# One-hot rows sent with the mask constants, identity sent alone, first head's rows copied on chip

## The chip, the cores and the metric

The kernel runs on one core of a Trainium2 chip. The metric is the device time of one execution in microseconds (us); lower is better. Three runs of the kernel before gave 269.93, 270.38 and 272.29 us, a median of 270.38 us. Engines are named as the profile names them: PE is the matrix engine (PEld is its weight load), DVE the vector engine, ACT the scalar engine, POOL the GpSimd engine, and SP the engine that does nothing here but issue transfers. ACT and POOL issue transfers as well, between their own work.

## The reference

The program is a block-sparse attention whose output goes through a token-and-channel mixer:

```python
scores = scale * np.matmul(q, k.transpose(0, 1, 3, 2))      # 4 batches, 8 heads, 768 x 64
mask = np.abs(blk_i - blk_j) <= 1                             # blocks of 32: the neighbours,
mask = mask | (blk_i == 0) | (blk_j == 0) | (blk_i == last) | (blk_j == last)
mask[qb's rows, kb's columns] = True                          # and three sampled blocks per row block
attn = softmax(np.where(mask, scores, -1e9))
x = concat_heads(attn @ v)                                    # 4 x 768 x 512
u = x + (x.T @ U @ V).T
out = u + np.maximum(u @ w_ch1, 0.0) @ w_ch2
```

The part that matters here is how the mask gets into the scores. There are 24 blocks of 32 tokens, so the mask is a 24 x 24 table. For the first batch the kernel adds it by widening the inner product: beside the 64 rows of a head's queries stand 24 rows that are one-hot (row i is 1 where the token lies in block i), and beside the 64 rows of its keys stand 24 rows that hold the bias of that key against each query block. One matrix product of 128 rows then gives score plus bias.

## The kernel before

Eight heads of a batch are worked in four pairs; there are sixteen pairs in all. For a pair the kernel turns queries and keys so that the head dimension lies on partitions, multiplies key tiles of 128 tokens by all 768 queries (lines 980, 999 and, from batch 1 on, 1030), takes the exponential on ACT (989, 1007, 1039), and multiplies by the values (414). The mixer's products (685, 760) are woven between. The order of all of that is written out by hand in a string of words (line 448 on), and each engine runs its instructions strictly in program order. Semaphores hold an instruction until what it needs is there.

The change lies in the prologue, lines 243 to 342, also in a fixed order. The tile `res` holds, for two sets, the widened queries `qres` and keys `kres` of two heads each: 128 partitions, 768 columns of 16-bit numbers per head. For head 0 of a pair, partitions 0 to 63 hold data and 64 to 87 the mask rows; for head 1 the data lies on 64 to 127 and the mask rows on 0 to 23. Unused rows are zero.

What the prologue does, engine by engine:

- SP issues the loads of head 0's queries and keys (line 182), then two copies of the one-hot rows from DRAM into set 0 (line 187, `one_hot(0, 1)` and `one_hot(0, 0)`), each behind the DVE memset of the rows that it writes into, then head 1's queries and keys, the values of pair 0, and pair 1's loads (153, 166). Later, in `second_set` (192 to 196), it writes set 1's one-hot rows, again from DRAM, copies the key mask rows from set 0, and fills `kmask`.
- ACT issues two transfers: `small` (line 245; a 128-row tile with the fixed part of the mask `ms`, the block numbers `iota` and a 128 x 128 identity `id16`), and the sampled blocks `sb` (246). Then it loads its function table and runs one small exponential (265).
- DVE zeroes five regions, casts head 0's queries (213), works out the mask bias from `sb`, `iota` and `ms` (302, 306, 309) and casts head 0's keys.
- POOL zeroes set 1 with two memsets over all 128 partitions (261), sets the columns of ones in the value tiles (263), and casts head 1's queries and keys when they land.
- PE runs eight products whose results nobody uses (`keep_warm`, 272), turns head 0's queries with `id16` (227), multiplies the bias by head 1's one-hot rows (`mask_half`, 279), turns the keys, and goes on to the first scores. ACT and DVE move these results out of PSUM (`first_row` 293, `mask_row` 287).

A transfer issued from SP or ACT takes one of eight semaphore lanes in turn, and its issue waits for the landing of the transfer eight places before it.

Of the kernel before, what the change touches and what calls it, by code (L numbers as in the profile page):

```python
# [12 lines left out]
FP32 = mybir.dt.float32  # L13
FP16 = mybir.dt.float16
# [5 lines left out]
P = 128  # L20
# [3 lines left out]
def kernel(  # L24
# [14 lines left out]
    nc = tc.nc  # L39

    B, H, S, D = q.shape
    BLK = 32
    NB = S // BLK
# [9 lines left out]
    MASK_BIAS = -240.0  # L53
# [3 lines left out]
    ii = np.arange(NB)  # L57
    ms_np = (
        (np.abs(ii[None, :] - ii[:, None]) <= 1)
        | (ii[None, :] == 0)  # L60
        | (ii[:, None] == 0)
        | (ii[None, :] == NB - 1)
        | (ii[:, None] == NB - 1)
    ).astype(np.float32)
    cols = np.arange(S)
    blk = ((cols % P) * T + cols // P) // BLK
    ohT_np = (blk[None, :] == ii[:, None]).astype(np.float16)
    small_np = np.zeros((P, NB + 1 + P // 2), np.float32)
    small_np[:NB, :NB] = (ms_np - 1.0) * -MASK_BIAS
    small_np[:NB, NB] = ii  # L70
    small_np[:, NB + 1 :] = np.eye(P, dtype=np.float16).view(np.float32)

    small_dr = nc.inline_tensor(small_np, name="small_const")
    ohT_dr = nc.inline_tensor(ohT_np, name="one_hot_const")

    consts = ctx.enter_context(tc.tile_pool(name="consts", bufs=1))
    wpool = ctx.enter_context(tc.tile_pool(name="wpool", bufs=1))
# [11 lines left out]
    def bank(n, shape, dtype):  # L89
        ap = PS[:, n, :]  # L90
        if dtype != FP32:
            ap = ap.bitcast(dtype)
        ap = ap[:, 0 : int(np.prod(shape[1:]))]
        return ap.rearrange("p (a b) -> p a b", a=shape[1]) if len(shape) > 2 else ap
# [3 lines left out]
    def psc2():  # L98
        ring["psc"] += 1
        return PS[:, (0, 3)[ring["psc"] % 2] :][:, 0:2]  # L100

    small = consts.tile([P, NB + 1 + P // 2], FP32)
    ms = small[0:NB, 0:NB]
    iota = small[0:NB, NB : NB + 1]
    id16 = small[:, NB + 1 :].bitcast(FP16)
    sb = consts.tile([P, NB, 3, 2], I32)
    vts = [consts.tile([P, H, T, DV], FP16, name=f"vt{i}") for i in range(2)]
    NEST = 16
# [3 lines left out]
    res = consts.tile([P, 4, 2, S], FP16, name="res")  # L112
    qres = [res[:, i] for i in range(2)]
    kres = [res[:, 2 + i] for i in range(2)]
    drows = [slice(0, D), slice(D, P)]
    mrows = [slice(D, D + NB), slice(0, NB)]
    hid = consts.tile([P, 2, 16, HS], FP16, name="hid")
# [58 lines left out]
    def first_load(h, n, queue):  # L176

        src, nm = ((q, "qld"), (k, "kld"))[n]
        if h == 0:
            lds[nm] = ldpool.tile([P, 2, T, D], FP32, tag="ld" + nm, name=nm)  # L180
            sts[0, nm] = stpool.tile([P, T, 2, D], FP16, tag="st" + nm, name="st" + nm)
        queue.dma_start(
            out=lds[nm][:, h], in_=src[0, h].rearrange("(p t) d -> p t d", t=T)
        )

    def one_hot(i, h):
        nc.sync.dma_start(out=qres[i][mrows[h], h, :], in_=ohT_dr.ap())

    warm = nc.const_aps.tensor(1.0, [P, 512], mybir.dt.bfloat16)
    bias = consts.tile([P, 2, D], FP16)  # L190

    def second_set():
        for h in range(2):
            one_hot(1, h)
            nc.sync.dma_start(out=kres[1][mrows[h], h, :], in_=kres[0][mrows[h], h, :])
        nc.sync.dma_start(out=kmask[mrows[0], :], in_=kres[0][mrows[0], 0, :])

# [13 lines left out]
    def first_cast(h, n, copy):  # L211
        nm = ("qld", "kld")[n]
        copy(out=sts[0, nm][:, :, h], in_=lds[nm][:, h])
# [3 lines left out]
    def first_turn(n, c):  # L217

        if n == 1:
            pt = bank(5 + c, [P, HS], FP32)  # L220
        elif c == 0:
            pt = pw[:, 1, 0:HS]
        else:
            pt = psc2()[:, 0, 0:HS]
        first_out[n, c] = pt
        for j in range(3):
            nc.tensor.matmul(
                pt[0:D, j * P : (j + 1) * P],
                sts[0, ("qld", "kld")[n]][:, 3 * c + j, 0],
                id16,  # L230
                start=(j == 0), stop=(j == 2), skip_group_check=True,
            )

    with tc.manual_schedule(
        engines={
            mybir.EngineType.PE,
            mybir.EngineType.DVE,
            mybir.EngineType.Activation,
            mybir.EngineType.SP,
            mybir.EngineType.Pool,  # L240
        }
    ):
        first_load(0, 0, nc.sync)
        first_load(0, 1, nc.sync)
        nc.scalar.dma_start(out=small, in_=small_dr.ap())
        nc.scalar.dma_start(
            out=sb[0:NB].rearrange("k z r w -> k (z r w)"),
            in_=sampled_blocks.bitcast(I32)
            .rearrange("z r -> (z r)")[None, :]
            .broadcast_to([NB, NB * 6]),  # L250
        )
        for h in (1, 0):
            nc.vector.memset(qres[0][(slice(D, P), slice(0, D))[h], h, :], 0.0)
            one_hot(0, h)
        nc.vector.memset(bias, 0.0)
        for h in range(2):
            nc.vector.memset(kres[0][(slice(D, P), slice(0, D))[h], h, :], 0.0)
        for n in range(2):
            first_load(1, n, nc.sync)
        for tile_ in (qres[1], kres[1]):  # L260
            nc.gpsimd.memset(tile_.bitcast(FP32), 0.0)
        for vt in vts:
            nc.gpsimd.memset(vt[:, :, :, D : D + 1], 1.0)
        first = consts.tile([P, 1], FP32)
        nc.scalar.activation(
            out=first, in_=nc.const_aps.tensor(1.0, [P, 1], FP32), func=AF.Exp
        )
        pw = psc2()

        def keep_warm(n, cols=512):  # L270
            for _ in range(n):
                nc.tensor.matmul(  # L272
                    pw[:, 0, 0:cols], warm[:, 0:P], warm[:, 0:cols], start=True, stop=True
                )

        pks = [bank(2, [P, HS], FP32), bank(7, [P, HS], FP32)]

        def mask_half(c):
            nc.tensor.matmul(
                pks[c],  # L280
                bias[0:NB].rearrange("k a z -> k (a z)"),
                qres[0][mrows[1], 1, c * HS : (c + 1) * HS],
                start=True, stop=True,
            )

        def mask_row(h, c, copy, lo=0, hi=HS):
            copy(
                out=kres[0][mrows[h], h, c * HS + lo : c * HS + hi],
                in_=pks[c][mrows[h], lo:hi],
            )  # L290

        def first_row(n, c, copy, lo=0, hi=HS):
            copy(
                out=(qres, kres)[n][0][drows[0], 0, c * HS + lo : c * HS + hi],
                in_=first_out[n, c][0:D, lo:hi],
            )

        neq = consts.tile([P, NB, 3], FP32)
        a01 = consts.tile([P, NB], FP32)
        keep_warm(8)  # L300
        first_cast(0, 0, nc.vector.tensor_copy)
        nc.vector.tensor_tensor(
            out=neq[0:NB], in0=sb[0:NB, :, :, 0],
            in1=iota[:, :, None].broadcast_to([NB, NB, 3]), op=ALU.not_equal,
        )
        nc.vector.tensor_reduce(
            out=a01[0:NB], in_=neq[0:NB], axis=mybir.AxisListType.X, op=ALU.min
        )
        nc.vector.scalar_tensor_tensor(
            out=bias[0:NB, :, 0:NB], in0=a01[0:NB, None].broadcast_to([NB, 2, NB]),  # L310
            scalar=MASK_BIAS, in1=ms[:, None].broadcast_to([NB, 2, NB]),
            op0=ALU.mult, op1=ALU.max,
        )
        first_turn(0, 0)
        first_row(0, 0, nc.scalar.copy)
        first_turn(0, 1)
        first_row(0, 1, nc.scalar.copy)
        first_cast(0, 1, nc.vector.tensor_copy)
        mask_half(0)
        mask_row(0, 0, nc.vector.tensor_copy, 0, P)  # L320
        mask_row(1, 0, nc.scalar.copy)
        first_turn(1, 0)
        first_row(1, 0, nc.vector.tensor_copy, 0, P)
        first_row(1, 0, nc.scalar.copy, P, HS)
        mask_row(0, 0, nc.vector.tensor_copy, P, HS)
        first_turn(1, 1)
        first_row(1, 1, nc.vector.tensor_copy)
        mask_half(1)
        mask_row(0, 1, nc.vector.tensor_copy)
        mask_row(1, 1, nc.vector.tensor_copy)  # L330

        for n in range(2):
            first_cast(1, n, nc.gpsimd.tensor_copy)
        for tile_ in (Vt, kmask):
            nc.gpsimd.memset(tile_.bitcast(FP32), 0.0)
        nc.vector.memset(Ut, 0.0)
        load_v(0)
        load_qk(1)
        load_v(1)
        load_mix_u()  # L340
        second_set()
        load_mix_v()

# [840 lines left out]
```

## Time and profile before

| what | value |
|---|---|
| profiled execution, its own time | 270.01 us |
| its span, first to last instruction | 268.2 us |
| runs: lowest, median, highest | 269.93, 270.38, 272.29 us |
| PE busy | 262.4 us, 98% of the span |
| DVE busy | 232.5 us, 87% |
| ACT busy | 202.7 us, 76% |
| POOL busy | 72.7 us, 27% |
| mean granted PE clock | 0.999 |

Busy time is the union of the intervals in which an engine has an instruction in flight. Products overlap in PE, so a busy PE need not be PE at its best. The profile also gives a chain of work that ended last: followed back from the last instruction, at each step to what released it. A timeline gives each instruction's start, its length, and in brackets the idle time before it and what ended that; SPq and ACTq rows are the issues of transfers. The trace also records every increment of a transfer's semaphore; the last of these is called its landing here. All times in a row count from the span's start.

### The profile page before, as it was taken

The page shows a single profiled execution, that of the slowest core. Times are in us where ns is not written, and L with a number is a line of the kernel's source. Part 1 is how long each engine was busy: PE and PEld are TensorE (multiplying, and loading weights), DVE is VectorE, ACT ScalarE, POOL GpSimd, SP SyncE. Part 2 cuts the span into 40 slices and gives each one's busy share as a digit, 9 for nine tenths or more (in the row PEclk, how much of TensorE's full clock was granted, in tenths as well). Part 3 has the DMA queues.
Part 4 walks back from the last instruction along what each step waited for, and adds up shares of the span by engine and source line. Part 5 has one row for each costly group of instructions (what it writes and reads, how often), then busy time and mean ns, then how long its engine had stood idle before and what let it go on. Part 6 is the DMA issues. An engine that isn't in the chain of part 4 may idle for free.

```text
span 268.2 us, 7303 instructions
## 1 busy us (share of the span) xinstructions
PE 262.4 (98%) x3006; PEld 182.4 (68%) x3006; DVE 232.5 (87%) x477; ACT 202.7 (76%) x265; POOL 72.7 (27%) x98
## 2 busy tenths in 40 slices
PE   8899999999999999999999999999999999999995
PEld 3677775555577778565666887555667788666884
DVE  5789988988999998868588997688998999999993
ACT  4999998897989667788898857788997944789200
POOL 4669006944462570070606160000000000000000
PEclk9999999999999999999999999999999999999999
DMA  6799997999999999897938997610200116400024
GB/s 192 245 324 263 207 235 123 113 135 144 189 146 133 117 103 111 284 98 89 90 39 67 106 109 139 223 34 13 51 0 2 42 42 117 159 2 0 2 98 137
DMA packets 88720, 31.66 MB, mean 118 GB/s; under 512 B 77104, under 2 KB 85840, under 8 KB 88688
## 3 DMA queue, kind: packets, MB, share of 16 engines
q0 software_dynamic: 49728, 10.10, 48.4%
q1 hardware_dynamic: 38492, 20.86, 33.6%
q8 instruction: 23, 0.38, 0.6%
q10 hardware_dynamic: 468, 0.26, 0.4%
q14 instruction: 9, 0.07, 0.1%
HBM read 27.67 MB, written 6.29 MB: 127 GB/s over the span
## 4 chain that ended last, share of the span: by engine, by line
PE 73%; DMA 12%; DVE 7%; ACT 2%; POOL 2%; issue 1%; SPq 0%; DVEq 0%; POOLq 0%; ACTq 0%
PE ps L760 32%; PE ps L685 17%; DMA w2t<-in_moe_w_ch_dram 9%; PE ps L414 9%; PE ps L1030 7%; DMA vld<-in_v_dram 2%; PE ps L999 2%; ACT est L1007 2%; PE ps L980 1%; DVE est L1045 1%; PE ps L272 1%; DMA qpl<-stqld 1%; PE ps L665 1%; DVE xf L551 1%; DVE res L969 1%
## 5 line engine op out<-in xcount | busy, mean ns | idle before, releaser
L1039 ACT ACTIVATE est<-ps 128x1536 f16<-128x1536 f32 x72 | 100.6, 1450 | 18.8 <-PE ps L1030 18.7
L685 PE MATMUL ps<-uT,w1t 128*128 128x384 f16 x384 | 70.2, 326 | 0.0
L1045 DVE TENSOR_TENSOR est<-est,mask 128x1440 f16<-128x1440 f16 x72 | 63.4, 903 | 0.6 <-ACT est L1039 0.2
L685 PEld LDWEIGHTS <-w1t 128*128 128x128 f16 x384 | 35.6, 97 | 26.6 <-issue 6.8
L414 PEld LDWEIGHTS <-est 128*128 128x128 f16 x1152 | 40.4, 97 | 7.0 <-issue 3.3
L414 PE MATMUL ps<-vt,est 128*128 128x65 f16 x1152 | 43.3, 193 | 0.2 <-DVE xf L551 0.2
L760 PEld LDWEIGHTS <-hid 128*128 128x128 f16 x358 | 34.0, 98 | 6.6 <-issue 1.6
L697 ACT ACTIVATE hid<-ps 128x384 f16<-128x384 f32 x63 | 29.7, 496 | 4.8 <-PE ps L685 4.3
L1030 PE MATMUL ps<-qpl,kpl 64*128 64x512 f16 (+1 forms) x288 | 31.7, 325 | 0.0
L139 POOL DMA_DIRECT2D stqld<-in_q_dram x20 | 16.3, 820 | 55.9 <-DMA qpl<-stqld 54.4
L760 PE MATMUL ps<-w2t,hid 128*128 128x256 f16 x238 | 31.1, 273 | 0.0
L879 DVE TENSOR_TENSOR xf<-xf,ps 128x256 f32<-128x256 f32 x63 | 25.4, 416 | 4.1 <-PE ps L760 3.7
L699 DVE TENSOR_SCALAR hid<-ps 128x384 f16<-128x384 f32 x33 | 18.3, 555 | 8.7 <-PE ps L685 8.0
L760 PEld LDWEIGHTS <-sums 128*128 128x128 f16 x216 | 20.1, 98 | 4.4 <-issue 1.0
L989 ACT ACTIVATE est<-ps 128x768 f16<-128x768 f32 x30 | 22.5, 812 | 0.1
L1030 PEld LDWEIGHTS <-kpl 64*128 64x128 f16 x288 | 12.3, 94 | 14.3 <-issue 9.1
L760 PE MATMUL ps<-res,sums 128*128 128x256 f16 x144 | 19.4, 273 | 0.0
L634 ACT CAST xh<-xf 128x384 f16<-128x384 f32 x24 | 11.0, 510 | 10.0 <-DVE xf L630 10.0
L551 DVE TENSOR_TENSOR xf<-ps,rcp 128x384 f32<-128x384 f32 x32 | 17.7, 554 | 0.8
L139 POOL DMA_DIRECT2D stkld<-in_k_dram x20 | 16.3, 819 | 1.9 <-issue 0.8
L139 POOL DMA_DIRECT2D vt<-in_v_dram x20 | 16.3, 820 | 0.0
L760 PE MATMUL ps<-res,hid 128*128 128x256 f16 x120 | 15.9, 273 | 0.0
(121 smaller groups left out, 339.3 us busy)
## 6 DMA issues: line engine op xcount, KB each, us to landing
out_dram<-xf SPq DMA_DIRECT2D x18, 256.0 KB, 2.4
vld<-in_v_dram SPq DMA_DIRECT2D x6, 384.0 KB, 6.3
w1t<-in_moe_w_ch_dram POOLq DMA_DIRECT2D x4, 512.0 KB, 8.3
w2t<-in_moe_w_ch_dram POOLq DMA_DIRECT2D x4, 512.0 KB, 12.1
qld<-in_q_dram SPq DMA_DIRECT2D x5, 384.0 KB, 3.7
kld<-in_k_dram SPq DMA_DIRECT2D x5, 384.0 KB
stqld<-in_q_dram POOLq DMA_DIRECT2D x20, 96.0 KB, 3.9
stkld<-in_k_dram POOLq DMA_DIRECT2D x20, 96.0 KB, 4.2
```

What stands on the lines that cost most here:

```text
L139: nc.gpsimd.dma_start(out=dst[:, h], in_=src[b, 2 * hp + h].rearrange("(p t) d -> p t d", t=T),)
L414: nc.tensor.matmul(pav[:, sc, :], est[:, n, sc * P : (sc + 1) * P], vts[b % 2][:, 2 * hp + h, g, 0 : D + 1], start=(g == 0 and sc == 0), s ...
L551: nc.vector.tensor_tensor(out=dst, in0=pav[:, :, 0:D], in1=rcp[:, :, None].broadcast_to([P, T, D]), op=ALU.mult,)
L685: nc.tensor.matmul(pt, w1t[:, cc, jj * P : (jj + 1) * P], bts[b].uT[:, cc, c * HS : (c + 1) * HS], start=(cc == 0), stop=(cc == NCC - 1), ...
L697: nc.scalar.activation(out=dst, in_=pt, func=AF.Relu)
L699: nc.vector.tensor_scalar_max(out=dst, in0=pt, scalar1=0.0)
L760: nc.tensor.matmul(acc[key], lhsT, rhs, start=(first and i == 0), stop=(i == len(pairs_) - 1), skip_group_check=True,)
L879: nc.vector.tensor_add(out=x, in0=x, in1=acc[a, b, tau])
L989: lambda: nc.scalar.activation(out=dst, in_=ps, func=AF.Exp, scale=0.125),
L1030: nc.tensor.matmul(units[h][:, u * S + lo : u * S + hi], kT[drows[h], g * P : (g + 1) * P], qT[drows[h], lo:hi], start=True, stop=True, sk ...
L1039: nc.scalar.activation(out=both[h], in_=units[h].rearrange("p (g n) -> p g n", g=2), func=AF.Exp, scale=0.125,)
L1045: lambda: nc.vector.tensor_mul(out=masked(both[h]), in0=masked(both[h]), in1=masked(mask[:, 2 * j : 2 * j + 2, :]),),
```

## The change

The one-hot rows, `ms` and `iota` become one DRAM constant of 32 rows, 1,636 bytes each, and ACT issues it in `small`'s place. It lands on partitions 0 to 31, in the columns of set 0's head 1 (the one-hot rows, and eight zero rows below them) and on into the first columns of set 1's head 0, where `ms` and `iota` stay until pair 1's queries are written there. The identity becomes a tile and a transfer of its own, the second on SP's queue. Head 0's one-hot rows in set 0 are no longer sent: ACT copies partitions 0 to 63 of head 1 to partitions 64 to 127 of head 0, behind its first exponential. Set 1's one-hot rows are copied from set 0 by transfers within the chip. One of DVE's memsets goes, another shrinks from 64 rows to 32; POOL's two memsets over 128 partitions and both heads become four over 64 partitions and one head.

```diff
+    NROW = 32
+    hot_np = np.zeros((NROW, S // 2 + NB + 1), np.float32)
+    hot_np[:NB, : S // 2] = (blk[None, :] == ii[:, None]).astype(np.float16).view(np.float32)
+    hot_np[:NB, S // 2 : S // 2 + NB] = (ms_np - 1.0) * -MASK_BIAS
+    hot_np[:NB, S // 2 + NB] = ii
+    hot_dr = nc.inline_tensor(hot_np, name="hot_const")
+    id_dr = nc.inline_tensor(np.eye(P, dtype=np.float16), name="identity_const")
...
-    small = consts.tile([P, NB + 1 + P // 2], FP32)
-    ms = small[0:NB, 0:NB]
-    iota = small[0:NB, NB : NB + 1]
-    id16 = small[:, NB + 1 :].bitcast(FP16)
+    id16 = consts.tile([P, P], FP16, name="id16")
...
+    hot = res.rearrange("p a b s -> p (a b s)")[:, S : 2 * S + 2 * NB + 2].bitcast(FP32)
+    ms = hot[0:NB, S // 2 : S // 2 + NB]
+    iota = hot[0:NB, S // 2 + NB :]
...
-    def one_hot(i, h):
-        nc.sync.dma_start(out=qres[i][mrows[h], h, :], in_=ohT_dr.ap())
+    def second_hot(h):
+        nc.sync.dma_start(out=qres[1][mrows[h], h, :], in_=qres[0][mrows[h], h, :])
...
     def second_set():
         for h in range(2):
-            one_hot(1, h)
+            second_hot(h)
...
         first_load(0, 0, nc.sync)
+        nc.sync.dma_start(out=id16, in_=id_dr.ap())
         first_load(0, 1, nc.sync)
-        nc.scalar.dma_start(out=small, in_=small_dr.ap())
+        nc.scalar.dma_start(out=hot[0:NROW], in_=hot_dr.ap())
...
-        for h in (1, 0):
-            nc.vector.memset(qres[0][(slice(D, P), slice(0, D))[h], h, :], 0.0)
-            one_hot(0, h)
+        nc.vector.memset(qres[0][NROW:D, 1, :], 0.0)
...
         for tile_ in (qres[1], kres[1]):
-            nc.gpsimd.memset(tile_.bitcast(FP32), 0.0)
+            for h in range(2):
+                nc.gpsimd.memset(tile_[drows[1 - h], h, :].bitcast(FP32), 0.0)
...
+        nc.scalar.copy(out=qres[0][drows[1], 0, :], in_=qres[0][drows[0], 1, :])
         pw = psc2()
```

## The prediction

> **What bounds the kernel now.** I read the page's slices first, then the chain of work over the prologue, then the timeline, and last the landing of each prologue transfer in the trace's semaphore record. The slices show that PE is at work from the second slice on, while the transfer engines are nearly full in the first third:
>
> ```profile
> PE   8899999999999999999999999999999999999995
> ...
> DMA  6799997999999999897938997610200116400024
> ```
>
> So this change can only act on when PE's work starts, or on a transfer that PE waits for. The chain says what the start hangs on (start, length, engine, tile and line):
>
> ```profile
> 0.78 3.57 PE ps L272 x8
> 4.35 0.47 PE ps L227 x3
> ...
> 4.84 0.85 ACT res L293 x2
> 5.69 0.46 ACT res L287
> ...
> 6.17 0.42 DVE res L287
> ...
> 6.62 0.55 DVE res L293
> ...
> 7.21 0.57 DVE res L287
> ...
> 7.82 0.82 PE ps L999 x4
> ```
>
> No transfer is in it. Eight products of `keep_warm` hold PE until about 4.2, then come the query turn, two copies and a mask row on ACT, three copies on DVE. The change edits none of these; it edits what must be there when they arrive. The question is how much room each input has.
>
> Landings before (last increment of each semaphore): `small` 3.22, head 0's queries 3.45, `sb` 3.65, head 0's keys 4.09, one-hot rows of head 1 4.68 and of head 0 5.24, head 1's queries 5.74 and keys 6.24. The readers:
>
> ```profile
> 1.65 0.80 SPq L187 DMA_DIRECT2D res<-one_hot_const  x2
> ...
> 2.49 0.37 SPq L182 DMA_DIRECT2D qld<-in_q_dram  x1
> ...
> 3.15 0.20 ACT L265 ACTIVATE first<-const-float32-1.0 128x1 f32<-128x1 f32 x1
> ...
> 3.75 0.22 DVE L302 TENSOR_TENSOR neq<-sb,small 24x72 f32<-24x72 int32 x1
> ...
> 4.28 0.77 PE L227 MATMUL ps<-small,stqld 128*64 128x128 f16 x6
> ...
> 4.84 0.85 ACT L293 CAST res<-ps 64x384 f16<-64x384 f32 x2 [1.49 <-PE ps L227]
> ...
> 4.98 0.33 PE L279 MATMUL ps<-res,bias 24*128 24x384 f16 x1
> 5.24 0.52 PE L227 MATMUL ps<-small,stkld 128*64 128x128 f16 x6
> ...
> 6.01 0.50 PE L980 MATMUL ps<-res 128*128 128x384 f16 x2
> ```
>
> Head 1's one-hot rows were there 0.30 before line 279 read them (4.98 - 4.68), head 0's 0.77 before the first score (6.01 - 5.24). Neither was late, so bringing them sooner frees nobody.
>
> **Identity, now on SP's queue.** It is issued second, at 1.20, where the keys were. From issue to landing, prologue transfers took between 2.48 (`small`, 0.74 to 3.22) and 3.33 us (head 1's keys, 2.91 to 6.24). That gives 3.68 to 4.53; line 227 wants it at 4.28, from a PE free at about 4.2. I take 3.7, by `small`, which also had 128 short rows, and so zero. At the far end the query turn, and all behind it, starts 0.25 us later.
>
> **Head 0's keys, one place later.** One issue on SP is 0.46 (0.74 to 1.20), so they are issued at 1.65; with the 2.89 that they took (1.20 to 4.09) they land at 4.54. Their cast now starts at 4.38 behind the bias on DVE and takes 0.34; it would start at 4.57 and end at 4.91, before the turn of the keys at 5.24: zero. With 3.33 they land at 4.98, the cast ends at 5.33, and the turn loses 0.1. Behind the cast on DVE waits line 287, but that waits for line 279 until 5.33 anyway.
>
> **One-hot rows with the constants.** ACT issues them at 0.74 as it issued `small`, and `sb` behind them at 1.13 as before. By the same two ends they land at 3.22 to 4.07. Three wait. DVE's `neq` starts at 3.75 behind the query cast (3.47 + 0.36 = 3.83, overlapped): the bias ends at 4.45, PE wants it at 4.98, so a landing up to 4.25 costs nothing. Line 279 itself wants the rows at 4.98. The third is the new copy on ACT. I take the low end, since the transfer stands first on its queue, as `small` did.
>
> The Trainium skill, page "DMA: Bandwidth & Descriptors", section "Why a DMA increments its semaphore by 16 and not by 1", says that a transfer from SP or ACT spreads over the largest number of engines up to 16 that divides its row count, the rest of the 16 being added at once. The trace agrees: the 24-row transfers show one early step (at 2.22 for the first one-hot copy) and then 12, the 128-row ones 16. By that rule 32 rows use all 16 engines with two packets each where `small` had eight, so the landing would be no later than 3.22, and the far end of 4.07 would fall out of the sum. The sum does not use this.
>
> **ACT's copy.** No row shows ACT copying 64x768 of 16-bit numbers from on-chip memory. Nearest: the exponential over 128x768 at 812 ns (line 989) and the cast of 128x384 at 510 ns (line 634), which doubled is 1.02 us. I take 0.85, nearer the row with the right length. It starts when the first exponential has ended (3.35) and the rows are there: 3.39 to 4.24. Queued behind it on ACT is line 293, which sits in the chain at 4.84 and has idled 1.49 us before it: room for 0.60. With the longest copy it ends at 4.41. It costs something only if the rows land after 3.97 (4.84 - 0.85 - 0.02); at 4.07, 0.12 us, with the longest copy 0.29. Its reader is the first score at 6.01.
>
> **Memsets.** DVE loses one memset of 0.38 and shortens none of the rest, since a memset's time goes by columns; it idles 0.52 until the queries land at 3.45, so nothing is won. POOL ran two of 0.74 each; four of half the columns are 0.37 each by those, or 0.42 each by line 335's 128x384: 1.48 to 1.68 in place of 1.47. POOL then waits until 5.79 (3.2 us idle): zero.
>
> **What SP's queue gains.** Two one-hot issues go (0.44 and 0.31, with gaps 0.84 from 1.65 to 2.49), one issue of 0.46 comes: head 1's loads and all up to `second_set` go out 0.38 earlier. Who takes it? POOL's casts of head 1 (5.79), read by PE at 8.48 behind its own earlier work; the values of pair 0, landed at 8.36, cast by 9.23, read at 9.63 in PE's order. None ended a wait of PE. And SP itself gives the lead back:
>
> ```profile
> 6.31 1.24 SPq L187 DMA_DIRECT2D res<-one_hot_const  x1
> ...
> 7.82 0.90 SPq L195 DMA_DIRECT2D res<-res  x1
> ...
> 8.77 0.52 SPq L187 DMA_DIRECT2D res<-one_hot_const  x1
> ```
>
> The row at 7.82 waits for DVE's mask row (7.77), which is in the chain and does not move. So a lead of 0.38 ends there, and from there on the issues follow one another.
>
> **Set 1's rows from on chip.** Their reader is pair 1's first score at 15.07; they landed at 12.83 and 13.23. The on-chip copies beside them took 0.77 and 0.90 to issue, the DRAM one at 8.77 took 0.52: up to 0.38 more for the one that is not covered by SP's wait. The transfer behind them is `kmask`, and it has no room: it landed at 13.59, and the product that reads it started right there:
>
> ```profile
> 11.22 1.45 ACT L1007 ACTIVATE est<-ps 128x1536 f16<-128x1536 f32 x1 [0.39 <-PE ps L999]
> ...
> 13.57 1.45 ACT L1007 ACTIVATE est<-ps 128x1536 f16<-128x1536 f32 x1 [0.20 <-PE ps L999]
> 13.63 0.34 PE L939 MATMUL ps<-res,kmask 128*128 128x384 f16 x1
> ```
>
> After that product PE's next wait is for ACT (1007 ends at 15.03, the next scores start at 15.07), and PE is through by about 14.84: 0.23 of room. On the other side, second-set transfers land one behind another, 0.2 apart (12.83, 13.04, 13.23, 13.41, 13.59), so they queue behind earlier traffic, which is now smaller and out sooner. Between +0.15 (0.38 - 0.23) and nothing I take nothing.
>
> **The sum** is 0.0 us on 270.01 (the profiled execution: a span of 268.2 and 1.8 around it). That execution lies 0.37 under the median of the runs, 270.38. For a median I forecast 270.2, midway.
>
> **Rivals.**
> 1. SP's lead reaches the end: 0.38 faster, 269.8 from 270.2. For it: the transfer engines are nearly full from 6 to 30 us, so work gone and started sooner lets everything land sooner, and `kmask` was awaited. Against it: no transfer in the chain before 34, and the wait at 7.82.
> 2. Slower: an input that had room comes late. The place is the identity at line 227: it lies behind the queries on one queue and decides from a landing of 4.23 on, 1:1, because the turn of the queries heads the chain; with the slowest landing 0.25 to 0.3, and `kmask` may add 0.15: 270.5 to 270.6. For it: one-hot rows in the same queue took 3.03 and 3.10 from issue to landing, by which the identity lands at 4.23 to 4.30, on the point itself. Against it: those had two loads of 128 long rows ahead, it has one.
> 3. ScalarE's copy becomes the bound: rows after 3.97. At most 0.29: 270.5.
>
> The Trainium skill, page "DMA: Bandwidth & Descriptors", section "Issuing engines are not separate DMA queues", says that transfers started from several engines share the same 16 and that spreading issues saves only issue time. By that rule moving the one-hot rows to ACT's queue could be worth no more than rival 1's 0.38. The record of landings agrees in so far as ACT's `sb` landed after SP's queries (3.65 against 3.45) though issued 0.39 behind them.
>
> **Chances.** The forecast 0.55, rival 1 0.14, rival 2 0.17, rival 3 0.04; 0.10 for what these rows do not show, such as another order of transfers in the crowded stretch to 75 us. About 1% (2.7 us) is what a measurement of this kernel can tell from no change. No rival reaches it; of the last tenth I give 0.03 to faster by more and 0.06 to slower by more. Within 1%: 0.91. The range takes in rivals 1 and 2 from the runs' own spread: 269.93 - 0.38 = 269.5 less 0.2 for a lower lowest, and 270.38 + 0.45 = 270.8 plus 0.4, since one of three runs lay 1.9 above: 269.3 to 271.2.
>
> **What would show it.** Right: the query turn still at 4.28, the first score at 6.0, 1007 at 8.7; ACT's copy between 3.4 and 4.3; the first row of `second_set` that waits for DVE still at 7.8. Wrong: a wait of line 227 for the identity, an ACT row 293 that starts directly behind the copy, or line 939 waiting past 13.8. The forecast fails by more than its range if a transfer in the crowded stretch changes place and a wait of PE opens there.

## The result, and the profile after

The changed kernel took 271.73 us (median of 22 runs, 270.26 to 274.16), the kernel before 270.38 (22 runs beside them, 269.65 to 272.29). The ratio is 1.004, with a 95% interval of 1.0023 to 1.0056: slower by about 1.1 us by this ratio (the medians lie 1.35 apart), within 1%, and 271.73 is above the top of my range, 271.2. The executions of both kernels fall into two heaps some 1.3 us apart, and why they do is a part of the answer below.

The profiled execution of the changed kernel took 272.00 us with a span of 270.2, against 270.01 and 268.2: 1.99 to explain. Its page, with the span, the busy times and the chain's shares by engine:

```profile
span 270.2 us, 7304 instructions
...
PE 264.3 (98%) x3006; PEld 183.3 (68%) x3006; DVE 232.3 (86%) x476; ACT 203.8 (75%) x266; POOL 72.9 (27%) x100
...
PEclk9999999999999999999999999999999999999999
...
PE 76%; DVE 8%; ACT 3%; issue 1%; DVEq 0%; ACTq 0%
```

The slices and the shares give no place. I compared the starts of the same exponentials on ACT in both traces, since they stand through the whole kernel: the first is late by 1.15 (7.70 against 6.54), the fourth by 1.48 (10.16 against 8.68), and this stays at 1.48 until 30.68; the 27th, at 33.22 against 31.34, is late by 1.88, and one near the end still by 1.91 (249.52 against 247.61). So the loss has two places only: the prologue with 1.48, and one point near 31 us with 0.4.

**The prologue.** The timeline of the changed kernel (start, length, engine, line, operation, tiles; in brackets the idle time before and what ended it):

```profile
1.21 0.41 SPq L244 DMA_DIRECT2D id<-identity_const  x1
1.66 0.43 SPq L182 DMA_DIRECT2D kld<-in_k_dram  x1
...
3.37 0.83 ACT L268 COPY res<-res 64x768 f16<-64x768 f16 x1
...
4.28 0.85 PE L227 MATMUL ps<-id,stqld 128*64 128x128 f16 x6
4.84 0.85 ACT L294 CAST res<-ps 64x384 f16<-64x384 f32 x2 [0.64 <-PE ps L227]
...
5.22 0.36 DVE L213 CAST stkld<-kld 128x384 f16<-128x384 f32 x1 [0.78 <-DMA kld<-in_k_dram]
5.63 0.85 PE L227 MATMUL ps<-id,stkld 128*64 128x128 f16 x6
...
6.84 2.10 PE L981 MATMUL ps<-res 128*128 128x384 f16 x6
7.70 2.21 ACT L990 ACTIVATE est<-ps 128x768 f16<-128x768 f32 x3 [0.81 <-PE ps L981]
8.16 0.73 SPq L195 DMA_DIRECT2D res<-res  x1
8.73 1.40 PE L1000 MATMUL ps<-res 128*128 128x512 f16 x4
...
10.16 1.45 ACT L1008 ACTIVATE est<-ps 128x1536 f16<-128x1536 f32 x1 [0.25 <-PE ps L1000]
```

The keys' cast, the first exponential and the fourth before:

```profile
4.38 0.34 DVE L213 CAST stkld<-kld 128x384 f16<-128x384 f32 x1
...
6.54 2.23 ACT L989 ACTIVATE est<-ps 128x768 f16<-128x768 f32 x3
...
8.68 1.45 ACT L1007 ACTIVATE est<-ps 128x1536 f16<-128x1536 f32 x1
```

Up to the cast of the queries' rows on ACT at 4.84 all is where it was before. Then DVE waits 0.78 for head 0's keys, which landed at 5.20 in place of 4.09; their cast starts at 5.22 in place of 4.38, their turn on PE at 5.63 in place of 5.24, the first score at 6.84 in place of 6.01. And PE is slower from there: the four products of line 1000 take 1.40, where before they took 0.82 (line 999, at 7.82). The trace's clock record has PE's full clock granted from 9.90 on, in the profile before from 4.83 on. The windows of the two traces show it by counts. The columns are the stretch, its length, the busy time of PE, PEld, DVE, ACT and POOL with the instructions in brackets, the clock, the DMA share and GB/s. Before:

```profile
8.60:9.80 1.20, 1.20 (x21) 0.90 (x19) 0.76 (x3) 1.20 (x2) 0.63 (x1) 1.00 1.01 375
```

After:

```profile
8.60:9.80 1.20, 1.20 (x6) 0.60 (x4) 0.46 (x2) 1.20 (x2) 0.71 (x1) 1.00 1.04 374
```

PE is busy for all of the 1.20 in both, with 21 products before and 6 after. The clock column reads 1.00 in both, as the page's PEclk row reads 9 throughout: neither shows a clock that has not been granted for the first time yet. Only the lengths of like products and the record of grants do.

**The point near 31 us.** DVE in the changed kernel:

```profile
29.94 0.56 DVE L616 TENSOR_TENSOR xh<-xh,ps 128x384 f16<-128x384 f16 x1
30.41 0.55 DVE L617 TENSOR_TENSOR xf<-xf,ps 128x384 f32<-128x384 f32 x1
31.40 0.56 DVE L616 TENSOR_TENSOR xh<-xh,ps 128x384 f16<-128x384 f16 x1 [0.44 <-issue]
```

The same three in the kernel before, one line number lower:

```profile
28.46 0.56 DVE L615 TENSOR_TENSOR xh<-xh,ps 128x384 f16<-128x384 f16 x1
28.94 0.55 DVE L616 TENSOR_TENSOR xf<-xf,ps 128x384 f32<-128x384 f32 x1
29.52 0.56 DVE L615 TENSOR_TENSOR xh<-xh,ps 128x384 f16<-128x384 f16 x1
```

DVE stands still for 0.44 us with nothing awaited ("issue"), where before it went on after 0.04 (28.94 + 0.55 = 29.49, then 29.52). The instruction does wait on ACT's semaphore, but the last increment ahead of its start came at 30.82, before the pause began at 30.96. It is the 64th entry of DVE's record in the changed kernel and the 66th before: the change took two entries out of DVE's stream (547 against 549 in the traces), a memset and one wait ahead of the copies of line 969. The list of DVE's waits holds it as one line, and it is easily passed over there:

```profile
DVE xh L616 <- issue: 0.4, 1, 0.4
```

Followed back from the last instruction, the chain after reaches no further than this place, with the pause as an entry; the chain before reaches back to 0.73:

```profile
30.96 0.44 issue
31.40 0.56 DVE xh L616
```

### The profile page after: what moved, and what is told of

Same layout as the page of the kernel before. It is cut to its first block, busy times and chain, and to the rows that moved or that the text cites. A ratio compares the mean times of both kernels' runs of the same rounds, so it can differ in the third digit from the quotient of the medians.

```text
span 270.2 us, 7304 instructions
## 1 busy us (share of the span) xinstructions
PE 264.3 (98%) x3006; PEld 183.3 (68%) x3006; DVE 232.3 (86%) x476; ACT 203.8 (75%) x266; POOL 72.9 (27%) x100
## 4 chain that ended last, share of the span: by engine, by line
PE 76%; DVE 8%; ACT 3%; issue 1%; DVEq 0%; ACTq 0%
PE ps L761 31%; PE ps L686 22%; PE ps L1031 9%; PE ps L415 9%; ACT est L1040 2%; DVE est L1046 2%; PE ps L981 1%; DVE xf L552 1%; DVE xf L880 1%; DVE sums L856 1%; DVE sums L722 1%; PE ps L666 1%; DVE hid L722 1%; ACT hid L698 1%; PE ps L1000 0%
```

## The experiments

Four theories, whose letters the first expectations use. **L**: head 0's keys land late because they are now the third transfer on SP's queue. **C**: PE's full clock comes late because PE stands idle while it waits for the keys. **F**: DVE's pause comes from the place of its instructions in its stream. **R**: the rest of the change costs the time (ACT's copy, set 1's rows, POOL's four memsets). The kernel before ran beside every batch, with medians of 270.14 to 270.28.

### The identity and the keys in other places

**e1.** The identity issued by ACT ahead of the one-hot rows, so that the keys are second on SP's queue:

```diff
-        nc.sync.dma_start(out=id16, in_=id_dr.ap())
         first_load(0, 1, nc.sync)
+        nc.scalar.dma_start(out=id16, in_=id_dr.ap())
         nc.scalar.dma_start(out=hot[0:NROW], in_=hot_dr.ap())
```

> The changed kernel, but the identity is issued by ACT, ahead of the one-hot rows, so head 0's keys are again the second transfer on SP's queue. Theory L (the keys' late landing, 5.20 against 4.09 before, is the cause): the keys' cast starts near 4.4, the first score near 6.0, and the time is that of the kernel before, ratio 0.998 to 1.001. Theory R (the rest of the change costs, the copies for set 1, POOL's memsets or ACT's copy): still 1.003 to 1.005.

Measured: 272.58 (6 runs), ratio 1.008 [1.005, 1.011]. The keys landed at 4.21, in time; but `sb`, now third on ACT's queue, landed at 5.37 in place of 3.62, and everything on DVE waited for it. The timeline:

```profile
5.47 0.22 DVE L303 TENSOR_TENSOR neq<-sb,res 24x72 f32<-24x72 int32 x1 [1.58 <-DMA sb<-in_sampled_blocks_dram]
...
6.37 0.34 DVE L213 CAST stkld<-kld 128x384 f16<-128x384 f32 x1
...
6.50 0.33 PE L280 MATMUL ps<-res,bias 24*128 24x384 f16 x1 [1.37 <-DVE bias L310]
```

The time missed what L gave, yet the same thing showed itself on another queue: there, too, the third transfer was the late one. PE's clock rose at 5.11 here, was taken back at 8.52 after the 1.37 of idleness, and came again at 11.93: both stretches are 3.41 long. The window at half clock, now shown since it follows a grant:

```profile
8.60:9.80 1.20, 1.20 (x5) 0.35 (x4) 1.14 (x3) 1.20 (x3) 0.98 (x2) 0.50 1.07 399
```

**e2.** SP's queue in the order queries, keys, identity:

```diff
-        nc.sync.dma_start(out=id16, in_=id_dr.ap())
         first_load(0, 1, nc.sync)
+        nc.sync.dma_start(out=id16, in_=id_dr.ap())
```

> The changed kernel, with queries, keys, identity in this order on SP's queue. Theory L: keys land near 4.1 and the ratio falls to 1.000 unless the identity, now third, lands after 4.25; if the third place is the slow one (its transfer takes 3.5 us, as the keys' did after the change), the identity lands near 5.1, the turn of the queries starts 0.8 late and the ratio is 1.003 to 1.006. Theory R: 1.003 to 1.005 with the query turn at 4.28.

Measured: 272.51 (12 runs), 1.0065 [1.003, 1.01]. Keys at 4.16, and now the identity, third, at 4.73:

```profile
4.77 0.78 PE L227 MATMUL ps<-id,stqld 128*64 128x128 f16 x6 [0.42 <-DMA id<-identity_const]
```

Here is the wait of line 227 that my second rival had described, with the transfer in another place. Whichever of the two stands third, PE waits for it.

**e6.** The identity issued by POOL:

```diff
-        nc.sync.dma_start(out=id16, in_=id_dr.ap())
+        nc.gpsimd.dma_start(out=id16, in_=id_dr.ap())
```

> The changed kernel with the identity issued by POOL ahead of its memsets, so that SP's queue has queries and keys first and ACT's queue the one-hot rows and sampled blocks, two transfers ahead of the prologue's needs on each. Theory L (the third place is the cause): keys land near 4.1, sampled blocks near 3.7, first score near 6.0, and only DVE's pause at 31 us stays: ratio about 1.0015. Theory R (ACT's copy, set 1's rows or the memsets cost too): above 1.003 with the first score at 6.0 and the loss between 7 and 29 us.

Measured: 271.29, 1.0015 [0.999, 1.0039]. Keys at 4.35 in time; but DVE's cast of the queries took 0.63 in place of 0.36 (3.82 to 4.45), so their turn came at 4.59, the keys' cast at 4.99 in place of 4.38, and the first score at 6.95, not near 6.0 as expected. The full clock came at 9.99 in the profiled execution, and DVE's pause was there. The median has the ratio that L gave, but the prologue does not look as L had it.

### The keys late in the kernel before

**e3.** An unused 128x128 transfer between queries and keys, so that the kernel before has its keys third:

```diff
...
         first_load(0, 0, nc.sync)
+        nc.sync.dma_start(out=extra, in_=extra_dr.ap())
         first_load(0, 1, nc.sync)
```

> The kernel before, with one transfer added: a 128x128 identity of 16-bit numbers that nothing reads, between the queries and the keys on SP's queue. Theory L: the keys land near 5.2, the first score moves from 6.0 to about 6.8, PE's full clock is granted later in many executions, ratio 1.003 to 1.005, as the whole change. Theory R: within 1.001 of before.

Measured: 270.84 (12 runs, 270.03 to 271.5), 1.0009 [0.9988, 1.003]. The profiled execution shows the picture of the changed kernel: keys landed at 5.14, the full clock came at 10.06, the exponentials 1.4 to 1.7 late.

```profile
5.16 0.36 DVE L215 CAST stkld<-kld 128x384 f16<-128x384 f32 x1 [0.60 <-DMA kld<-in_k_dram]
...
5.43 0.47 PE L282 MATMUL ps<-res,bias 24*128 24x384 f16 x1 [0.30 <-DMA res<-one_hot_const]
...
5.83 0.85 PE L229 MATMUL ps<-small,stkld 128*64 128x128 f16 x6
```

So one more transfer ahead of them is enough to make the keys late, with none of the rest of the change; L's mechanism stands. The delay behind it is not the keys' alone, though: head 1's one-hot rows were pushed back as well, to 5.39, and the mask product that PE runs ahead of the keys' turn waited 0.30 for them. There was no step at 31 us and no pause on DVE. In the time the median was 0.6 up, but the interval includes 1, and the ratio is below the 1.003 to 1.005 that L asked for.

**e7.** The same delay without a transfer, by a DVE memset of 0.75 ahead of the keys' cast:

```diff
+        nc.vector.memset(hid[:, 0, 0:4].bitcast(FP32), 0.0)
         first_cast(0, 1, nc.vector.tensor_copy)
```

> The kernel before with one memset of 0.75 us on an unused tile put ahead of DVE's cast of head 0's keys: the keys are late by about 0.8 as after the change, and no transfer is touched. Theory L: first score near 6.8, full clock at 4.8 in some executions and at 8 to 10 in others, ratio 1.002 to 1.004. If late keys cost nothing by themselves and the transfers behind them do: within 1.001.

Measured: 270.92 (270.15 to 273.34), 1.0014 [0.9988, 1.004]; cast at 5.20, turn at 5.54, clock at 10.20. Again the profile shows the exponentials 1.1 to 1.7 late, and the runs are spread over both heaps; the ratio is below the expected 1.002 to 1.004.

### A product of `keep_warm` in the gap

**e4.** One more product ahead of the turn of the keys, in the changed kernel:

```diff
         mask_row(1, 0, nc.scalar.copy)
+        keep_warm(1)
         first_turn(1, 0)
```

> The changed kernel with one more product of keep_warm (512 columns, result unused) between the mask product and the keys' turn, where PE stood idle for some 0.3 us. Theory C (most of the loss is PE's clock, which the idle time keeps at half until 9.9 where it rose at 4.8 before): the rise comes back to 4.8 to 6.5 and the ratio falls to about 1.001 to 1.002, the direct delay of the keys (0.4 us) staying. If the clock's rise has nothing to do with the idle time: 1.004 to 1.005.

Measured: 270.84 (270.4 to 271.49), 1.002 [1.0001, 1.0039]. In its profile the clock came at 4.27 and the exponentials stood within 0.2 of before until 29 us, though the keys landed at 5.00; from the pause on, 0.3 to 0.5 late. One profile with an early clock does not show that the product made it so: the next kernel has no such product and its clock came at 4.37.

### DVE's pause: the two entries given back, and taken away elsewhere

**e5.** Two memsets of an unused tile of one column on DVE, in the changed kernel:

```diff
...
         nc.vector.memset(bias, 0.0)
+        for _ in range(2):
+            nc.vector.memset(idle, 0.0)
```

> The changed kernel with two one-column memsets of an unused tile added to DVE's prologue, so that DVE's program has as many instructions ahead of pair work as before the change. In the profiles of the changed kernel DVE stands still for 0.44 us at its 64th instruction (near 31 us), with nothing awaited; in the kernel before that instruction is another one and no such pause is there. Theory F (the pause hangs on the position of the instruction in DVE's stream, which the change moved by two): the pause goes, the shift against before no longer grows by 0.4 at 31 us, ratio 0.0015 below the changed kernel's 1.004. If the pause comes from the data or the transfers: it stays, 1.004.

Measured: 270.34 (270.06 to 271.49), 0.9994 [0.9974, 1.0013]. More work, and the pause is gone. DVE's stream has 549 entries again, and the same add, now the 66th, follows after 0.04:

```profile
29.08 0.55 DVE L620 TENSOR_TENSOR xf<-xf,ps 128x384 f32<-128x384 f32 x1
29.66 0.55 DVE L619 TENSOR_TENSOR xh<-xh,ps 128x384 f16<-128x384 f16 x1
```

The keys were still late (5.08), the clock came at 4.37, and the exponentials were 0.25 late at first and 0.14 from 20 to 80 us: that is what late keys cost when the clock comes early.

**e10.** The reverse, in the kernel before: its four DVE memsets over 64 rows and one head (0.38 each) merged into two over 128 rows and both heads (0.70 each), nothing else.

```diff
+        nc.vector.memset(qres[0], 0.0)
         for h in (1, 0):
-            nc.vector.memset(qres[0][(slice(D, P), slice(0, D))[h], h, :], 0.0)
             one_hot(0, h)
...
-        for h in range(2):
-            nc.vector.memset(kres[0][(slice(D, P), slice(0, D))[h], h, :], 0.0)
+        nc.vector.memset(kres[0], 0.0)
```

> The kernel before with DVE's four prologue memsets over 64 rows drawn together into two over 128 rows (the same regions of zeros and the same total time), so that DVE's program is two instructions shorter, as after the change, and nothing else differs. Theory F: the pause of 0.44 us appears at DVE's 64th instruction near 29.5 us, and the exponentials behind it come 0.4 later than before: ratio 1.001 to 1.002. If the pause belongs to the changed transfers: no pause, ratio within 1.001.

Measured: 270.51 (270.06 to 271.98), 1.0005 [0.9989, 1.0022]. Two entries fewer, and the pause stands in the kernel before:

```profile
29.17 0.55 DVE L615 TENSOR_TENSOR xf<-xf,ps 128x384 f32<-128x384 f32 x1
30.16 0.56 DVE L614 TENSOR_TENSOR xh<-xh,ps 128x384 f16<-128x384 f16 x1 [0.45 <-issue]
```

Its exponentials are 0.24 late until 29 us and 0.64 at the 27th: the step of 0.4 at the same place. F is shown in both directions, by the profile; 0.44 us (0.16%) is less than the run's interval can tell.

### Both mended, and the changed kernel again

**e8.** The identity by POOL and the two DVE memsets together:

```diff
...
-        nc.sync.dma_start(out=id16, in_=id_dr.ap())
+        nc.gpsimd.dma_start(out=id16, in_=id_dr.ap())
...
+        for _ in range(2):
+            nc.vector.memset(idle, 0.0)
```

> The changed kernel with the identity issued by POOL and the two small memsets on DVE, both suspected causes taken away at once. Theory L and F together explain the loss: ratio 0.998 to 1.001. Something else costs as well: 1.002 or more.

Measured: 270.39, 1.0001 [0.9979, 1.0023]; keys 4.14, first score 6.15, no pause, the clock at 4.86. Nothing is left that the time can tell, and R finds no support. But not every cause is gone: as in e6, DVE's cast of the queries was slow (0.83) and the keys' cast came at 4.99, late though the keys had landed. In both, POOL's memsets, pushed back by its issue of the identity (from 1.96 on, in the changed kernel from 0.73), were still running then; whether they slow the cast was not tried.

**e9.** The changed kernel unchanged, in a later batch:

> The changed kernel once more, on the same chip as the three that follow. The pause at DVE's 64th instruction is in its profile again (0.44 us near 30 us); ratio 1.002 to 1.006. If the clock's rise falls where it may, about half of its executions lie 1 us or more above its fastest.

Measured: 270.84 (270.56 to 272.85), 1.0034 [1.0011, 1.0057]; seven of 12 runs between 270.56 and 270.87, five above 271.5. Here the clock came at 5.83, the keys landed at 4.69, and the exponentials were 0.2 to 0.4 late before the pause and 0.5 to 0.6 behind it.

**e11 and e12.** The product of `keep_warm` together with the two DVE memsets in the changed kernel, and that product alone in the kernel before (the two memsets as in e5):

```diff
...
+        keep_warm(1)
         first_turn(1, 0)
```

> The changed kernel with the two small DVE memsets and one more product of keep_warm ahead of the keys' turn: the pause gone, and PE kept at work while it waits for the keys. If late keys cost mostly through PE's clock: fewer executions 1 us above the fastest, ratio 0.998 to 1.000. If not: as the run with the two memsets alone, 0.999 to 1.001.

> The kernel before with one more product of keep_warm ahead of the keys' turn. The keys are on time there, so the product delays their turn: by 0.43 us at half clock, 0.21 at full clock. If the kernel before already has its clock early in nearly all executions: ratio 1.000 to 1.002. If a fifth of its executions rise late and the product keeps PE busy for them: 0.998 to 1.000.

Measured: 270.63, 1.0006 [0.9985, 1.0027], and 270.23, 0.9998 [0.9977, 1.002]. The first had keys at 5.26 and a first score at 6.96, the product having pushed the turn to 6.03; its clock came at 6.51. No version beats the kernel before.

### The two causes apart, on one chip

The earlier batches ran on different chips, so the four combinations ran together on one: **f1** is the changed kernel (both causes), **f2** that of e5 (late keys only), **f3** that of e10 (pause only), **f4** that of e8 (neither). The letters A, B, C are those of these expectations.

> The changed kernel itself, one of four kernels of one chip in which VectorE's pause and the late keys are present or absent: here both. Theory A (the pause of 0.44 us and the late keys each cost their part, and add up): 1.0035 to 1.0045 of the kernel before. Theory B (only the pause costs): 1.0016, as much as the kernel with the pause alone. Theory C (only the late keys cost, by the clock): the pause in the profile, the time as the kernel with late keys alone. In the profile: keys land 4.7 to 5.3, the pause of 0.44 before VectorE's 64th instruction. If TensorE's clock is granted at boundaries 3.41 us apart whose place against the start is a matter of chance, the full clock begins either between 4.2 and 6.2 or between 9.4 and 10.5, and the time is about 1.3 us longer in the second case.

> The changed kernel with two memsets of an unused tile of one column on VectorE: late keys, no pause. Theory A: 1.002 to 1.003 of the kernel before. Theory B: 1.000. Theory C: as the changed kernel, 1.004. In the profile: keys land 4.7 to 5.3, no pause; the full clock from 4.2 to 6.2 or from 9.4 to 10.5, as for the changed kernel.

> The kernel before with its four memsets of 64 rows on VectorE merged into two of 128 rows: the pause, no late keys. Theory A: 1.0016. Theory B: as the changed kernel. Theory C: 1.000. In the profile: keys land 4.1 to 4.3, the pause of 0.44 before VectorE's 64th instruction.

> The changed kernel with the identity issued by GpSimd and two memsets of an unused tile on VectorE: keys second on SP's queue, so in time, and no pause. All three theories: 1.000 of the kernel before; anything above is a cost of the rest of the change (ScalarE's copy, the second set's rows, GpSimd's memsets) or of the identity's place. In the profile: keys land 4.1 to 4.4, no pause, first score 6.0 to 6.2.

Measured against 270.14 of 35 runs: 1.0018 [0.9996, 1.004], 1.0004 [0.9982, 1.0027], 1.0024 [0.9997, 1.0051], 1.0004 [0.9977, 1.0031]. The intervals overlap, and no theory is chosen by them. The pause was in the first and third trace (0.44 and 0.45) and in neither of the others; the third shows its cost most plainly, with exponentials 0.02 late up to 29 us and 0.43 from the 27th on. The last kernel is the surprise: its keys landed at 4.17, in time, and its clock still came at 9.84. Its first score, at 6.91, missed the 6.0 to 6.2 expected.

```profile
3.64 0.81 DVE L214 CAST stqld<-qld 128x384 f16<-128x384 f32 x1 [1.07 <-DMA qld<-in_q_dram]
...
4.98 0.34 DVE L214 CAST stkld<-kld 128x384 f16<-128x384 f32 x1
...
6.91 2.10 PE L984 MATMUL ps<-res 128*128 128x384 f16 x6
...
8.80 1.32 PE L1003 MATMUL ps<-res 128*128 128x512 f16 x4
```

The changed kernel, in the same batch, had its keys at 5.14 and the clock at 5.17:

```profile
5.16 0.36 DVE L213 CAST stkld<-kld 128x384 f16<-128x384 f32 x1 [0.52 <-DMA kld<-in_k_dram]
...
6.31 1.45 PE L981 MATMUL ps<-res 128*128 128x384 f16 x6
```

So late keys are not enough for a late clock, and C as I had it falls. Whether some delay of them is needed, f4 does not show: its keys landed in time, but their cast, behind the slow cast of the queries, began 0.6 later than before (4.98 against 4.38). e8 had the same late cast (4.99) and its clock at 4.86. (One grant, 3.57 in the second kernel, also lay below the 4.2 I had expected as the least.)

### All runs together

A line at 271.15 parts the two heaps roughly. It is my choice, from the gap in the times of the kernel before. Medians of the executions below it:

| kernels | below 271.15 | share above |
|---|---|---|
| before, five batches | 270.09 to 270.31 | 33 of 156 |
| keys landed in time, no pause (both mended twice, fill in before) | 270.14 to 270.20 | 9 of 36 |
| late keys or late cast, no pause (e3, e5, e7, f2) | 270.17 to 270.34 | 15 of 48 |
| pause, no late keys (e10, f3) | 270.51, 270.62 | 4 of 24 |
| both: changed kernel, three batches | 270.75, 270.69, 270.73 | 15 of 22, 5 of 12, 3 of 12 |

(The variants that make something else late, e1, e2 and e6, and those with a product in the changed kernel, e4 and e11, are left out.)

In the lower heap, each against the kernel before of its own batch, the pause costs 0.35 to 0.53 and late keys about 0.1 to 0.2, and together they make the changed kernel's 0.44 to 0.64. Most of the upper heap fits the late clock: of the 18 profiles, the five with a grant at 9.84 to 10.20 took 271.50 to 272.09 and none of them less, while those with a first grant at 6.51 or earlier took 270.01 to 271.24, but for the two kernels in which the identity or `sb` was late. No execution of the kernel before in its upper heap was profiled, and one of f1 lies above the line (271.24) with an early clock. There the loss is at another place, an input of the mixer that landed late:

```profile
DVE w2t L722 <- DMA w2t<-in_moe_w_ch_dram: 0.7, 1, 0.7
```

DVE waits 0.67 for it up to 75.69, PE then 0.7 for DVE, and the exponentials, 0.6 late until then, are 1.06 late from 85 us on. e2's trace has the same wait. So the share above the line is only roughly the share of late clocks, the more so as the pause lifts all times of a kernel by 0.4 and the line stays.

## Why the prediction was wrong

**Right.** The one-hot rows landed at 3.02, no later than the 3.22 taken; ACT's copy ran from 3.37 for 0.83 (predicted 3.39 and 0.85), and line 294 behind it still idled 0.64; the identity landed at 3.80 (3.7 taken); the query turn stood at 4.28; POOL's memsets took 1.81, a little over the 1.68 given, with 2.7 of idleness behind them. Rival 1 did not come, and SP's lead (3.12 against 3.38) was lost even earlier than I had it: the first row of `second_set` went out at 6.63, before at 6.31, ahead of the row that waits for DVE (8.16 against 7.82). Rival 3 did not come. (Its prices were 0.02 too high: a landing at 4.07 gives 0.10, with the longest copy 0.27.) Set 1's rows left no mark: from the fourth to the 26th exponential the distance of the two kernels stays at 1.48.

Within 1% was the outcome that I gave 0.91, but the time lies past the range, on the slower side, to which I had given somewhat more (rivals 2 and 3, 0.21) than to the faster (rival 1, 0.14). Of the signs that I had named for being right, the first score (6.84 for 6.0) and line 1007 (10.16 for 8.7) failed.

The sum was 0.0, and three terms that it put at nothing were not: DVE's shorter stream, the keys' later place, and the time at which PE's clock rises. The first two explain the lower heap, whose median of 270.75 would have lain in the range. What carried the median past 271.2 is the upper heap, with 15 of the 22 executions; why there were so many stays open.

**Wrong, the memsets on DVE.** "DVE loses one memset of 0.38 and shortens none of the rest … so nothing is won": I priced the time of the memset and took a shorter stream for free. It cost 0.44, and e5 and e10 show that the number of entries ahead of it does it, whichever kernel has it. This was no rival and no part of the bounds; it could only have stood in the tenth for what the rows do not show. The profile of before has no row for it: at that add it has a gap of 0.04.

**Wrong in size, the keys one place later.** The step said that they land at 4.54 by 2.89 from issue to landing, at 4.98 by the longest transfer of the prologue (3.33), with 0.1 lost at the far end. They took 3.54 and landed at 5.20; in the changed kernel's other two profiles 5.14 and 4.69, in the variants that kept its order on SP 5.00 to 5.26. The bound came from transfers issued later or with other shapes, and it was no bound: what was issued around 1.65 had its own row, the one-hot copy of 1.65 that landed at 4.68, and I read its 3.03 for the identity, which did not stand there, and not for the keys, which did. By it the keys would have landed at 4.68 and lost nothing, so even that row was short of 5.20. The cause of the slow landing behind 1.6 us is not settled.

**Wrong by omission, the clock.** The sum had PE's products at one speed. The 1.15 to 1.48 in the prologue of the profiled execution are 0.39 at the turn of the keys, and the rest products at half rate until 9.90. It is not a price that the changed kernel alone pays: by its times the kernel before seems to pay it in some 33 of 156 executions, and f4, whose keys landed in time and were cast late, paid it too. What the change did to its frequency stays open. It was 15 of 22 against 2 of 22 in the comparison that gave the result, which moves that median by 0.98 (271.73 against 270.75 in the lower heap), but 5 of 12 against 10 of 35, and 3 of 12 against 5 of 35, in two later batches. All three point the same way (23 of 46 against 17 of 92), but the first carries most of it. With e3 and e7, where late keys without the rest of the change gave 11 of 24, a higher share is plausible, and e5 and f2, with 4 of 24, do not show it.

**The rivals and the range.** Rival 2 had the right kind (an input that had room comes late) and the wrong input (the identity, not the keys). It named 270.5 to 270.6, near the lower heap's 270.7, of which only some 0.15 has the reason that it gave. The range ended at 271.2 because the upper heap had shown itself in one of the three runs given (272.29), which I took for a stray and gave only part of its distance.

## What to carry to other kernels

A change that takes instructions out of an engine's stream moves all later instructions of this engine to other places in it; look in the profile after for a new idle time that nothing ended ("issue"), and try whether idle instructions put back remove it. Price a transfer's landing by the rows that were issued at the same moment, not by its old duration carried to a later place. Where the starting clock of PE decides on a microsecond, one profile and three runs cannot tell a change of that size from chance: compare heaps, and compare on one chip.

## What the runs showed of the hardware

**A pause at a fixed place of DVE's stream.** All nine traces in which DVE's record has 547 entries have a pause of 0.44 to 0.46 before the 64th, each time when a wait on a semaphore had just ended; none of the nine with 549 or 550 has one. The number 64 alone does not make it: in e7, with 550, the 64th entry is an add that starts without a pause. In the eight traces with 549 the 64th is that wait itself, which lasts 1.0 us (28.48 to 29.48 before), and in e7 the wait follows directly. So what would stop DVE there may pass unseen within the wait; 548 entries were not tried. The DMA record names packets of the kind "instruction", and those of 8,192 bytes move with it: the first after the prologue starts at 28.5 to 30.7 in the traces without the pause, within 0.9 us of DVE's 64th entry, and at 33.4 to 36.3 in those with it, 3 to 5 us behind that entry; a later one goes from 87.7 to 89.4 to 97.9 to 101.2. The Trainium skill, page "Runtime: NRT & Kernel Launch", section "Instruction fetch mechanics", says that an engine's instructions are refilled in blocks by transfers of its own and that crossing a block is mostly hidden. By that the pause would be a refill that was not hidden; the packets fit it, and no run here shows it, since which engine a packet serves is not in the record.

**Third transfers.** In the prologue the first two transfers of a queue took 2.3 to 3.2 us to land; the third one that an engine issued, around 1.65, took 3.0 to 3.8 (the keys 3.03 to 3.61, the identity 3.07, `sb` 3.76, the one-hot rows before 3.03 to 3.63), and where head 1's queries stood there 3.4 to 4.2. That held on SP's and on ACT's queue. Third place and issue around 1.65 go together in all runs, so which of the two makes the landing late was not parted.

**PE's first full clock.** Eighteen profiles have the first grant between 3.57 and 6.51, or between 9.84 and 10.20. The late ones less 3.41 lie at 6.43 to 6.79. That looks like boundaries 3.41 us apart at a place of chance, where one that falls past about 6.4, right behind the gaps around the turn of the keys, is passed over; every first boundary up to 5.83 was taken. The one at 6.51 that was taken had the product of `keep_warm` in the gap. The Trainium skill, page "TensorE: Matmul & The Clock Gate", section "What's actually happening", has just such free-running windows of 3413 ns; the 3.41 of e1 agrees. It says that the ramp costs under 1% of a typical span: here a rise that comes late adds 1.3 us, 0.5% of the span, which does not contradict it, and yet that is more than the change itself costs in the lower heap. How much idleness makes a window fail was not found: by the trace's modelled ends, windows that failed had PE busy for 3.11 to 3.41 of the 3.41, and a window that was taken for as little as 2.80 (f2's, where the idleness lay ahead of PE's first product).
